# Attention followed by a gated convolution FFN on one core: a fixed order of the lead-in on three engines, weight casts in pieces, and the shifted V by DMA

## The chip, the core and the metric

The kernel runs on one core of a Trainium2 chip. The core has five engines that run side by side: TensorE (PE, matmuls; its weight loads are listed as PEld), VectorE (DVE), ScalarE (ACT), GpSimd (POOL) and SyncE (SP, which here only issues DMAs). The metric is the device time of one execution in microseconds, lower is better; a comparison takes the median of several runs.

## The reference

Eight batches of attention over a sliding window of 32 positions to each side, followed by a feed-forward layer with a convolution of width 3 along the sequence:

```python
# B, H, S, D = 8, 8, 576, 64;  d_model = 512, d_ff = 1024
scores = q @ k.T / sqrt(D)                    # per batch and head
scores = where(abs(i - j) <= 32, scores, -1e9)
attn   = softmax(scores)
x      = (attn @ v)  as [B, S, H * D]
h      = maximum(x @ w_in, 0)                 # [B, S, 1024]
conv   = sum_k conv_w[k] * h shifted by k - 1 # along S
gate   = 1 / (1 + exp(-conv))
out    = (h * gate) @ w_out                   # float32 [8, 576, 512]
```

## The kernel before

The kernel is written as a list of jobs, each with a planned time and the jobs it must follow. `give_out` takes them in the order of the planned times and emits their instructions; a scheduler may then move instructions of an engine past each other, unless they are wrapped in `fixed`, which keeps the program's order. The planned times are thus an order, not a clock.

A batch has four pair groups of heads (`g`). For each two groups `job_tr` transposes q and k on TensorE (the two engines ACT and DVE copy the halves out of PSUM), `job_sc` makes the scores of one group in a score buffer of which there is one, ACT takes the exponential, and DVE multiplies with the band mask. `job_av` multiplies with V. Half of the key tiles of V start 64 rows further down, so there are two copies of V in SBUF: `ve`, cast from the load, and `vo`, the same rows shifted by 64 partitions. `job_xt` transposes the result to the FFN's input, `job_ph` is the projection with `w_in`, `job_pc` the convolution (three matmuls with diagonal matrices `diag_w`) and the gate, and `job_py` the output projection.

```python
fixed = tc.keep_in_program_order

class InOrder:
    on = False
    def __getattr__(self, name):
        def give(*args, **kwargs):
            ins = getattr(nc.vector, name)(*args, **kwargs)
            return fixed(ins) if self.on else ins
        return give

vector = InOrder()                      # DVE alone; on for planned times under T0 + 14

def cast(out_, in_):                    # all casts of inputs and weights: POOL, in order
    fixed(nc.gpsimd.tensor_scalar(
        out=out_, in0=in_, scalar1=1.0, scalar2=0.0, op0=ALU.mult, op1=ALU.add))

def cast_v(c):                          # in load_stream(b)
    cast(ve[:, c, :, 0:64], vst[:, c, :, :])
    if b == 0 and c > 0:                # batch 0: shifted on DVE, block by block
        vector.tensor_copy(vo[0:64, c - 1, :, :], ve[64:128, c - 1, :, :])
        vector.tensor_copy(vo[64:128, c - 1, :, :], ve[0:64, c, :, :])

def shift_v(b):                         # the other batches: after the last cast of V
    ve, vo = ve_pp[b % NLD], vo_pp[b % NLD]
    for p0, src in ((0, ve[64:128, 0:NBLK - 1]), (64, ve[0:64, 1:NBLK])):
        if b == 1:
            vector.tensor_copy(out=vo[p0:p0 + 64], in_=src)
        else:
            fixed(nc.scalar.dma_start(vo[p0:p0 + 64], src))

def load_weight(src, dst, rows, cast_):
    n = src.shape[1] // 2
    for x in (0, n):                    # two halves: a load of 1 MB, and one cast
        ...
        yield load, lambda x=x, st=st: cast_(dst[:, :, x:x + n], st[0])

def make_diag(m):                       # three 128x128 matrices of one block m of 128 channels
    for kk in range(3):
        vector.tensor_scalar(out=diag_w[:, kk, m, :], in0=ident,
                             scalar1=conv_w_sb[:, kk, m:m + 1], scalar2=None, op0=ALU.mult)

def job_sc(g):
    ...
    ps, last = slot_a(), slot_f()       # slot_a: the one score buffer (three PSUM banks)
    ...                                 # 18 matmuls
    nc.scalar.activation(attn[:, 0:x], ps[:, 0:x], AF.Exp, bias=0.0, scale=scale)
    nc.scalar.activation(attn[:, x:], last[:, 0:64], AF.Exp, bias=0.0, scale=scale)
    vector.tensor_tensor(out=attn, in0=attn, in1=mask, op=ALU.mult)
```

The parts of the plan that belong to the lead-in (`b` is the batch, `g` the pair group, `c` a block of 128 rows, `m` a block of 128 channels):

```python
T0, T1 = 22.0, 42.5
hidden(0, T0, 1.6, None)                # chunk 0: job_ph at T0 + 1.6 m, job_pc at T0 + 1.6 (m + 1.4)
...
at(("diag", m), T0 + 1.6 * m - 1.0, ...)
# batch 0: transposes of q, of k; scores; attention times V
t0, t1, t2, t3 = 5.8 + 1.35 * (g // 2) * 2, 7.2 + 1.35 * (g // 2) * 2, 8.4 + 2.0 * g, 16.2 + g
at(("xt", b, c), ... if b else 20.3 + 0.4 * c, ...)
at(("vo", b), x + y + 1.5, lambda b=b: shift_v(b), ("cast", b, NV - 1))
at(("w_in", i), 16.5 + 2.0 * i, cs, ...)
at(("w_out", i), 34.0 + i, cs, ...)
```

Of the kernel before, what the change touches and what calls it, by code (L numbers as in the profile page):

```python
# [17 lines left out]
def kernel(  # L18
# [58 lines left out]
    class InOrder:  # L77


        on = False  # L80

        def __getattr__(self, name):
            def give(*args, **kwargs):
                ins = getattr(nc.vector, name)(*args, **kwargs)  # L84
                return fixed(ins) if self.on else ins

            return give

    vector = InOrder()

# [41 lines left out]
    def shift_v(b):  # L132

        ve, vo = ve_pp[b % NLD], vo_pp[b % NLD]
        for p0, src in ((0, ve[64:128, 0:NBLK - 1]), (64, ve[0:64, 1:NBLK])):
            if b == 1:
                vector.tensor_copy(out=vo[p0:p0 + 64], in_=src)
            else:
                fixed(nc.scalar.dma_start(vo[p0:p0 + 64], src))

# [42 lines left out]
    def load_weight(src, dst, rows, cast_):  # L183

        n = src.shape[1] // 2
        for x in (0, n):
            st = {}

            def load(x=x, st=st):
                t_ = fpool.tile([128, rows * n], FP32, name="wst", tag="wst")  # L190
                st[0] = t_.rearrange("p (c f) -> p c f", c=rows)
                fixed(nc.sync.dma_start(
                    st[0], src.rearrange("(c p) f -> p c f", p=128)[:, :, x:x + n]
                ))

            yield load, lambda x=x, st=st: cast_(dst[:, :, x:x + n], st[0])

# [10 lines left out]
    def job_tr(g2, y):  # L208

        b, i = g2 // NPH, g2 % NPH  # L210
        nat = qkb_pp[b % NLD][y][i]
        to = []
        for g in (2 * g2, 2 * g2 + 1):
            if y == 0:
                t_ = apool.tile([128, S], BF16, name="qT", tag="qT", bufs=4)
                to.append(t_)
            else:
                t_ = kT_pp[g % NKT]
                to.append(t_[:, PAD:PAD + S])
            state["qk"[y], g] = t_  # L220

        small = b == 0
        for js in ((range(0, 4), range(4, 8), range(8, RP)) if small else (range(RP),)):
            j0, n = js[0], len(js)
            ps = slot_f() if small else slot_a()
            for j in js:
                nc.tensor.matmul(  # L227
                    ps[:, 128 * (j - j0):128 * (j - j0) + 128],
                    nat[:, j, :, :].rearrange("p e d -> p (e d)"),
                    ident, start=True, stop=True,  # L230
                )
            rows = ps[:, 0:128 * n].rearrange("p (j y x) -> p y x j", j=n, y=2)
            for x, copy in enumerate((nc.scalar.copy, vector.tensor_copy)):
                copy(
                    out=to[x].rearrange("p (x j) -> p x j", j=RP)[:, :, j0:j0 + n], in_=rows[:, x]
                )

    def job_conv_w():
        ps = slot_f()
        nc.tensor.matmul(ps[:, 0:3 * MB], conv_w24, ident24, start=True, stop=True)  # L240
        vector.tensor_copy(out=conv_w_sb.rearrange("p k m -> p (k m)"), in_=ps[:, 0:3 * MB])
# [8 lines left out]
    def job_sc(g):  # L250
        qT, kT = state.pop(("q", g)), state.pop(("k", g))
        ps, last = slot_a(), slot_f()
        for i in range(NT):
            for e, t in ((0, (i + NT - 1) % NT), (1, i)):
                nc.tensor.matmul(  # L255
                    last[:, 0:64] if e * t == NT - 1 else ps[:, col(e, t):col(e, t) + 64],
                    kT[64 * e:64 * e + 64, 64 * t:64 * t + 128],
                    qT[64 * e:64 * e + 64, 64 * t:64 * t + 64],
                    start=True, stop=True,
                )  # L260
        attn = apool.tile([128, 2 * S], BF16, name="attn", tag="attn", bufs=4)
        state["a", g] = attn
        x = 2 * S - 64
        nc.scalar.activation(attn[:, 0:x], ps[:, 0:x], AF.Exp, bias=0.0, scale=scale)  # L264
        nc.scalar.activation(attn[:, x:], last[:, 0:64], AF.Exp, bias=0.0, scale=scale)  # L265
        vector.tensor_tensor(out=attn, in0=attn, in1=mask, op=ALU.mult)

    def job_av(g):
# [7 lines left out]
        for e in range(2):  # L276
            for c in range(NBLK):
                for j in range(2):
                    t = min(2 * c + j, NT - 1)
                    nc.tensor.matmul(  # L280
                        pss[e][64 * j:64 * j + 64, 65 * c:65 * c + 65],
                        attn[:, col(e, t):col(e, t) + 64],
                        (ve if t % 2 == 0 else vo)[:, t // 2, head(pr, e), :],
                        start=True, stop=True,
                    )
# [6 lines left out]
        for e, (po, rec, to) in enumerate(outs):  # L292
            if b == 0 and e == 1 and pr < 3:
                for c in range(NBLK):
                    nc.scalar.activation(
                        to[:, c, :], po[:, c, 0:64], AF.Copy, bias=0.0, scale=rec[:, c:c + 1]
                    )
# [6 lines left out]
    def job_xt(b, c):  # L304
# [5 lines left out]
        for kc in range(KC):  # L310
            nc.tensor.matmul(  # L311
                ps[:, kc, 0:cols],
                xn[b][:, c, 2 * kc:2 * kc + 2, :].rearrange("p h d -> p (h d)"),
                ident[:, 0:cols], start=True, stop=True,
            )
        (vector.tensor_copy if b > 1 or c % 2 else nc.scalar.copy)(
            out=xT[b // 2][:, :, b % 2, 128 * c:128 * c + cols], in_=ps[:, :, 0:cols]
# [13 lines left out]
    def job_ph(c, m, halves=(0, 1)):  # L331
# [8 lines left out]
        for kc in range(KC):  # L340
            nc.tensor.matmul(  # L341
                ps[:, 0:n], w_in_sb[:, kc, m * 128:(m + 1) * 128], x_[:, kc, x0:x1],
                start=(kc == 0), stop=(kc == KC - 1),
            )
        if kind == 1:
            out_ = hT[:, m, :].rearrange("p (i x) -> p i x", i=2)
            for i in halves:
                o_ = out_[:, i, i:i + HW + 1]
                i_ = ps[:, (HW + 1) * (i - halves[0]):(HW + 1) * (i - halves[0]) + HW + 1]
                if halves == (0, 1):  # L350
                    continue
                nc.scalar.activation(o_, i_, AF.Relu, bias=0.0, scale=0.5)
            if halves == (0, 1):
                base = hT[:, m, 0:HW + 1]
                both = bass.AP(base.tensor, base.offset, [list(base.ap[0]), [HW + 3, 2], [1, HW + 1]])
                nc.scalar.activation(
                    both, ps[:, 0:n].rearrange("p (i x) -> p i x", i=2), AF.Relu, bias=0.0, scale=0.5
                )
        else:
            o0 = 1 if kind == 0 else 0  # L360
            nc.scalar.activation(hT[:, m, o0:o0 + n], ps[:, 0:n], AF.Relu, bias=0.0, scale=0.5)  # L361

    def job_pc(c, m, halves=(0, 1)):
# [14 lines left out]
        for kk in range(3):  # L378
            nc.tensor.matmul(  # L379
                ps[:, 0:n], diag_w[:, kk, m, :], taps(kk), start=(kk == 0), stop=(kk == 2)  # L380
            )
        tn = spool.tile([128, CH], FP32, name="tn", tag="tn")
        nc.scalar.activation(tn[:, 0:n], ps[:, 0:n], AF.Tanh, bias=0.0, scale=1.0)  # L383
        vector.scalar_tensor_tensor(
# [8 lines left out]
    def job_py(c, i):  # L393

        ps = slot_f()
        for m in range(MB):
            nc.tensor.matmul(  # L397
                ps, gT[c][:, m, 128 * i:128 * i + 128], w_out_sb[:, m, :],
                start=(m == 0), stop=(m == MB - 1),
            )  # L400
        y_sb = spool.tile([128, d_model], FP32, name="y_sb", tag="y_sb", bufs=4)
        nc.scalar.copy(out=y_sb, in_=ps)  # L402
        r0 = c * CH + 128 * i
# [16 lines left out]
    def give_out():  # L420
# [9 lines left out]
        while ready:  # L430
            _, _, key = heapq.heappop(ready)
            vector.on = plan[key][0] < T0 + 14.0
            plan[key][1]()
# [7 lines left out]

    T0, T1 = 22.0, 42.5
    start = {0: T0, 1: T1}
# [21 lines left out]
    for m in range(MB):  # L465
        at(("diag", m), T0 + 1.6 * m - 1.0, lambda m=m: make_diag(m), ("conv_w",))
    at(("conv_w",), 7.0, job_conv_w)
# [26 lines left out]
    for g in range(NG):  # L494
# [4 lines left out]
        if b == 0:  # L499
            t0, t1, t2, t3 = 5.8 + 1.35 * (g // 2) * 2, 7.2 + 1.35 * (g // 2) * 2, 8.4 + 2.0 * g, 16.2 + g  # L500
        else:
# [9 lines left out]
    for b in range(B):  # L511
        t, d = pair[b * NP + NP - 1]
        for c in range(NBLK):
            at(("xt", b, c), t + (2.0 + 0.06 * c) * d if b else 20.3 + 0.4 * c, lambda b=b, c=c: job_xt(b, c),
               *[("av", b * NP + i) for i in range(NP)],
               *[("ph", (b // 2 - 2) * 3 + 2, m, None) for m in range(MB)])
        t0 = pair[b * NP][0]
        for i, (ld, cs) in enumerate(load_stream(b)):
            if b == 0:
                x, y = -20.0, 20 + (4.3 + 1.35 * i if i < NP else 9.8 + 1.1 * (i - NP))  # L520
            elif b == 1:
# [3 lines left out]
            else:  # L525
                x, y = t0 - P - 3.0 + i * P / NV, 4.5
            at(("load", b, i), x, ld if b else lambda: None, ("load", b, i - 1),
               *[("cast", b - 1, j) for j in range(NV)],
# [8 lines left out]
    for i, (ld, cs) in enumerate(load_weight(moe_w_in, w_in_sb, KC, cast)):  # L537
        at(("w_in load", i), -1.0, ld, *[("load", 0, j) for j in range(NV)])
        at(("w_in", i), 16.5 + 2.0 * i, cs, ("w_in load", i))
    for i, (ld, cs) in enumerate(load_weight(moe_w_out, w_out_sb, MB, cast)):  # L540
# [33 lines left out]
```

The softmax here doesn't subtract the row's maximum and nothing guards it: scores larger than these inputs give would overflow.

## Time and profile before

| | |
|---|---|
| median of 3 runs | 286.14 us (284.77 to 286.53) |
| span of the profiled execution | 282.2 us |
| PE busy | 246.8 us, 87% |
| DVE busy | 181.5 us, 64% |
| ACT busy | 175.9 us, 62% |
| POOL busy | 77.1 us, 27% |
| shift copies of V on DVE (`vo<-ve`) | 10, 290 to 2282 ns |
| shift DMAs of V on ACT's queue | 12, median 5.3 us from issue to landing |

How to read the profile: it is one execution, taken by the hardware profiler, and its times are microseconds from the start of the span. A group of instructions is written as line, engine, operation, output<-input, shape of each (partitions x elements) and count. In a timeline the first two numbers are the start and the length, and a bracket holds the idle time of the engine ahead of the group and what ended it. A table by stage has for each engine its busy time and, in brackets, its count of instructions; after the engines come TensorE's granted clock (1.00 is full speed), the share of the DMA engines and the rate in GB/s. L84 is the helper through which all DVE work of the jobs goes, so DVE's operations are told apart by their tiles; L109 is the cast on POOL. A matmul's end is modelled, so a busy PE is not PE at its peak.

### The profile page before, as it was taken

The page shows a single profiled execution, that of the slowest core. Times are in us where ns is not written, and L with a number is a line of the kernel's source. Part 1 is how long each engine was busy: PE and PEld are TensorE (multiplying, and loading weights), DVE is VectorE, ACT ScalarE, POOL GpSimd, SP SyncE. Part 2 cuts the span into 40 slices and gives each one's busy share as a digit, 9 for nine tenths or more (in the row PEclk, how much of TensorE's full clock was granted, in tenths as well). Part 3 has the DMA queues.
Part 4 walks back from the last instruction along what each step waited for, and adds up shares of the span by engine and source line. Part 5 has one row for each costly group of instructions (what it writes and reads, how often), then busy time and mean ns, then how long its engine had stood idle before and what let it go on. Part 6 is the DMA issues. An engine that isn't in the chain of part 4 may idle for free.

```text
span 282.2 us, 6681 instructions
## 1 busy us (share of the span) xinstructions
PE 246.8 (87%) x2652; PEld 152.2 (54%) x2682; DVE 181.5 (64%) x394; ACT 175.9 (62%) x370; POOL 77.1 (27%) x84
## 2 busy tenths in 40 slices
PE   1756767877999898999989999999989999999994
PEld 1535433656665554666555555565555655555551
DVE  5687989795465888486556767596656555733330
ACT  2755672565676666677765577766755677557652
POOL 5657738661026221043113412332200000000000
PEclk9999995797999999999999999999999999999999
DMA  6999999781687742784649564954240102011022
GB/s 231 253 329 360 210 365 256 193 280 32 171 207 239 199 114 66 231 272 118 148 95 310 156 161 131 306 165 114 65 115 37 39 37 78 37 39 74 37 78 112
DMA packets 55555, 45.58 MB, mean 162 GB/s; under 512 B 38860, under 2 KB 40932, under 8 KB 55524
## 3 DMA queue, kind: packets, MB, share of 16 engines
q1 hardware_dynamic: 54528, 41.95, 50.7%
q10 hardware_dynamic: 996, 3.21, 4.9%
q8 instruction: 21, 0.34, 0.6%
q14 instruction: 10, 0.08, 0.1%
HBM read 32.52 MB, written 9.44 MB: 149 GB/s over the span
## 4 chain that ended last, share of the span: by engine, by line
PE 70%; DVE 19%; ACT 5%; DMA 3%; issue 2%; SPq 1%; POOL 0%; DVEq 0%; ACTq 0%
PE pf L397 21%; PE pf L341 20%; PE pf L379 14%; PE pa L227 5%; PE pf L280 4%; DVE attn L84 3%; DVE xT L84 3%; DVE gT L84 3%; DMA kst<-in_k_dram 3%; DVE vo L84 3%; PE pa L255 3%; DVE diag_w L84 2%; ACT attn L264 2%; PE pf L311 2%; DVE xn L84 2%
## 5 line engine op out<-in xcount | busy, mean ns | idle before, releaser
L84 DVE SCALAR_TENSOR_TENSOR gT<-tn,hT 128x384 bf16<-128x384 f32 (+1 forms) x104 | 60.2, 587 | 43.2 <-ACT tn L383 42.9
L341 PE MATMUL pf<-xT,w_in_sb 128*128 128x385 bf16 (+2 forms) x416 | 81.3, 322 | 3.7 <-DVE xT L84 2.2
L379 PE MATMUL pf<-hT,diag_w 128*128 128x384 bf16 (+1 forms) x312 | 66.0, 320 | 2.6 <-DVE rec L84 1.5
L397 PE MATMUL pf<-w_out_sb,gT 128*128 128x512 bf16 x258 | 66.4, 380 | 1.6 <-issue 0.2
L383 ACT ACTIVATE tn<-pf 128x384 f32<-128x384 f32 (+1 forms) x104 | 49.0, 472 | 12.4 <-PE pf L379 11.8
L341 PEld LDWEIGHTS <-w_in_sb 128*128 128x128 bf16 x416 | 38.8, 100 | 27.1 <-DVE xT L84 2.0
L109 POOL TENSOR_SCALAR ve<-vst 128x512 bf16<-128x512 f32 x40 | 28.6, 719 | 60.8 <-DMA vst<-in_v_dram 37.7
L402 ACT COPY y_sb<-pf 128x512 f32<-128x512 f32 x36 | 21.1, 586 | 38.2 <-PE pf L397 35.8
L397 PEld LDWEIGHTS <-gT 128*128 128x128 bf16 x288 | 27.7, 98 | 29.3 <-issue 0.3
L361 ACT ACTIVATE hT<-pf 128x385 bf16<-128x385 f32 x64 | 31.8, 497 | 14.0 <-PE pf L341 13.4
L379 PEld LDWEIGHTS <-diag_w 128*128 128x128 bf16 x312 | 28.2, 99 | 20.9 <-issue 1.8
L264 ACT ACTIVATE attn<-pa 128x1088 bf16<-128x1088 f32 x32 | 34.5, 1079 | 7.2 <-PE pf L255 3.8
L84 DVE TENSOR_TENSOR attn<-attn,mask 128x1152 bf16<-128x1152 bf16 x32 | 27.1, 846 | 7.8 <-ACT attn L265 5.8
L109 POOL TENSOR_SCALAR qb<-qst 128x1152 bf16<-128x1152 f32 x16 | 19.3, 1204 | 35.6 <-DMA qst<-in_q_dram 32.5
L84 DVE TENSOR_TENSOR xn<-pf,rec 128x320 bf16<-128x320 f32 x61 | 27.8, 482 | 0.8 <-DVE rec L84 0.2
L84 DVE CAST xT<-pf 128x512 bf16<-128x512 f32 (+1 forms) x34 | 20.4, 634 | 9.6 <-PE pf L311 9.6
L109 POOL TENSOR_SCALAR kb<-kst 128x1152 bf16<-128x1152 f32 x16 | 19.1, 1194 | 19.1 <-DMA kst<-in_k_dram 12.2
L280 PEld LDWEIGHTS <-attn 128*64 128x64 bf16 x640 | 14.7, 119 | 16.5 <-issue 8.8
L280 PE MATMUL pf<-ve,attn 128*64 128x65 bf16 x384 | 19.2, 207 | 5.0 <-DVE attn L84 3.6
L255 PEld LDWEIGHTS <-kT 64*128 64x128 bf16 x576 | 12.7, 98 | 13.5 <-issue 6.7
L280 PE MATMUL pf<-vo,attn 128*64 128x65 bf16 x256 | 17.2, 207 | 3.0 <-DVE vo L84 3.0
L84 DVE RECIPROCAL rec<-pf 128x5 f32<-128x5 f32 x64 | 10.4, 181 | 14.1 <-PE pf L280 13.6
(54 smaller groups left out, 206.4 us busy)
## 6 DMA issues: line engine op xcount, KB each, us to landing
qst<-in_q_dram SPq DMA_DIRECT2D x16, 576.0 KB, 6.4
kst<-in_k_dram SPq DMA_DIRECT2D x16, 576.0 KB, 7.6
out_dram<-y_sb SPq DMA_DIRECT2D x36, 256.0 KB, 2.2
vst<-in_v_dram SPq DMA_DIRECT2D x24, 256.0 KB, 4.6
vo<-ve ACTq DMA_DIRECT2D x12, 260.0 KB, 5.3
vst<-in_v_dram SPq DMA_DIRECT2D x16, 192.0 KB, 4.6
wst<-in_moe_w_in_dram SPq DMA_DIRECT2D x2, 1024.0 KB, 8.3
wst<-in_moe_w_out_dram SPq DMA_DIRECT2D x2, 1024.0 KB, 9.5
```

Source lines behind the costliest of these rows:

```text
L84: ins = getattr(nc.vector, name)(*args, **kwargs)
L109: fixed(nc.gpsimd.tensor_scalar(out=out_, in0=in_, scalar1=1.0, scalar2=0.0, op0=ALU.mult, op1=ALU.add))
L227: nc.tensor.matmul(ps[:, 128 * (j - j0):128 * (j - j0) + 128], nat[:, j, :, :].rearrange("p e d -> p (e d)"), ident, start=True, stop=True,)
L255: nc.tensor.matmul(last[:, 0:64] if e * t == NT - 1 else ps[:, col(e, t):col(e, t) + 64], kT[64 * e:64 * e + 64, 64 * t:64 * t + 128], qT[ ...
L264: nc.scalar.activation(attn[:, 0:x], ps[:, 0:x], AF.Exp, bias=0.0, scale=scale)
L280: nc.tensor.matmul(pss[e][64 * j:64 * j + 64, 65 * c:65 * c + 65], attn[:, col(e, t):col(e, t) + 64], (ve if t % 2 == 0 else vo)[:, t // 2 ...
L341: nc.tensor.matmul(ps[:, 0:n], w_in_sb[:, kc, m * 128:(m + 1) * 128], x_[:, kc, x0:x1], start=(kc == 0), stop=(kc == KC - 1),)
L361: nc.scalar.activation(hT[:, m, o0:o0 + n], ps[:, 0:n], AF.Relu, bias=0.0, scale=0.5)
L379: nc.tensor.matmul(ps[:, 0:n], diag_w[:, kk, m, :], taps(kk), start=(kk == 0), stop=(kk == 2))
L383: nc.scalar.activation(tn[:, 0:n], ps[:, 0:n], AF.Tanh, bias=0.0, scale=1.0)
L397: nc.tensor.matmul(ps, gT[c][:, m, 128 * i:128 * i + 128], w_out_sb[:, m, :], start=(m == 0), stop=(m == MB - 1),)
L402: nc.scalar.copy(out=y_sb, in_=ps)
```

## The change

It has three parts. The helper that keeps the program's order is now used for TensorE, ACT and DVE alike, for all jobs with a planned time under T0 + 14, and the plan of the lead-in is written anew: the scores of batch 0's first two groups stand ahead of the transposes of the second two, three of the diagonal matrices are made early, the others later. The cast of each half of a weight is cut into four pieces of 128x512 elements. And the shifted V of all batches but the first comes by DMA on SP's queue, where batch 1 had it from DVE and the others from ACT's queue. The aim of the first part is a lead-in whose order is chosen and not left to the scheduler; of the second, that a weight's cast does not occupy POOL in one long operation; of the third, that neither DVE nor ACT's queue carries the shift.

```diff
+        def __init__(self, engine):
+            self.engine = engine
+
         def __getattr__(self, name):
-            ...
+            do = getattr(self.engine, name)
+            return (lambda *args, **kwargs: fixed(do(*args, **kwargs))) if InOrder.on else do
-    vector = InOrder()
+    vector, scalar, tensor = InOrder(nc.vector), InOrder(nc.scalar), InOrder(nc.tensor)
 ...  (in the jobs nc.tensor becomes tensor, and nc.scalar scalar)
         for p0, src in ((0, ve[64:128, 0:NBLK - 1]), (64, ve[0:64, 1:NBLK])):
-            if b == 1:
-                vector.tensor_copy(out=vo[p0:p0 + 64], in_=src)
-            else:
-                fixed(nc.scalar.dma_start(vo[p0:p0 + 64], src))
+            fixed(nc.sync.dma_start(vo[p0:p0 + 64], src))
 ...  (load_weight)
-            yield load, lambda x=x, st=st: cast_(dst[:, :, x:x + n], st[0])
+            def casts(x=x, st=st):
+                step = 512 // n
+                for c in range(0, rows, step):
+                    cast_(dst[:, c:c + step, x:x + n], st[0][:, c:c + step])
+
+            yield load, casts
 ...  (the plan)
-    T0, T1 = 22.0, 42.5
+    T0, T1 = 23.0, 43.0
-        at(("diag", m), T0 + 1.6 * m - 1.0, lambda m=m: make_diag(m), ("conv_w",))
+        at(("diag", m), (8.8, 9.0, 11.7)[m] if m < 3 else T0 + 1.6 * m - 1.5, lambda m=m: make_diag(m), ("conv_w",))
-            t0, t1, t2, t3 = 5.8 + 1.35 * (g // 2) * 2, 7.2 + 1.35 * (g // 2) * 2, 8.4 + 2.0 * g, 16.2 + g
+            t0, t1 = ((6.0, 7.5), (10.5, 12.2))[g // 2]
+            t2, t3 = (9.4, 10.4, 14.7, 16.2)[g], 18.0 + 0.8 * g
-  ("xt", b, c): 20.3 + 0.4 * c   for batch 0
+  ("xt", b, c): 21.5 + 0.3 * c
-                x, y = -20.0, 20 + (4.3 + 1.35 * i if i < NP else 9.8 + 1.1 * (i - NP))
+                x, y = -20.0, 20 + ((4.9, 6.4, 8.8, 10.9)[i] if i < NP else 12.1 + 1.25 * (i - NP))
-            at(("load", b, i), x, ld if b else lambda: None, ("load", b, i - 1),
+            at(("load", b, i), x, ld if b else lambda: None, ("load", b, i - 1), *[("vo", 1)][:b - 1],
-        at(("w_in", i), 16.5 + 2.0 * i, cs, ("w_in load", i))
+        at(("w_in", i), 17.2 + 1.0 * i, cs, ("w_in load", i))
```

The term added to `("load", b, i)` keeps the loads of batches 2 and later behind batch 1's shift on the queue.

## The prediction

> **What bounds the kernel now.** I first read the page's slices, to see where TensorE isn't full, and then the busy times by stage.
>
> ```profile
> PE   1756767877999898999989999999989999999994
> PEclk9999995797999999999999999999999999999999
> ...
> 30.00:40.00 10.00, 9.04 (x87) 5.22 (x88) 8.33 (x22) 7.45 (x16) 4.79 (x7) 1.00 1.03 287
> 40.00:52.00 12.00, 8.41 (x74) 4.82 (x74) 11.48 (x18) 3.99 (x8) 8.38 (x6) 0.60 0.88 250
> 52.00:70.00 18.00, 13.33 (x201) 11.13 (x201) 13.16 (x28) 12.07 (x29) 8.89 (x11) 0.89 0.58 177
> 70.00:283.00 213.00, 200.52 (x2075) 119.01 (x2102) 126.54 (x260) 136.72 (x279) 36.49 (x40) 1.00 0.46 131
> ```
>
> A slice is 7 us. From the fourteenth slice (92 us) on TensorE is at eight or nine tenths, and in the stage from 70 us it is busy for 200.5 of 213 us at full clock. What follows 70 us is TensorE's own work, and nothing in the change makes that smaller. So the change can win only before 70 us: each microsecond by which TensorE gets its full stream earlier is a microsecond off the end. The columns after the stage's length are PE, PE's weight loads, DVE, ACT, POOL, then the clock and the DMA share. The stage 40 to 52 stands out: DVE 11.48 of 12 us, ACT nearly idle, the clock at 0.60.
>
> Next the timeline of DVE and of POOL in that stage:
>
> ```profile
> 39.31 3.01 DVE L84 COPY vo<-ve 64x2080 bf16<-64x2080 bf16 x2
> 42.35 0.76 DVE L84 TENSOR_TENSOR attn<-attn,mask 128x1152 bf16<-128x1152 bf16 x1
> 43.02 4.12 DVE L84 TENSOR_SCALAR diag_w<-ident,conv_w_sb 128x128 bf16<-128x128 bf16 x3
> 47.06 0.55 DVE L84 SCALAR_TENSOR_TENSOR gT<-tn,hT 128x384 bf16<-128x384 f32 x1
> ```
> ```profile
> 39.62 2.15 POOL L109 TENSOR_SCALAR w_out_sb<-wst 128x2048 bf16<-128x2048 f32 x1 [3.94 <-DMA wst<-in_moe_w_out_dram]
> 42.60 2.27 POOL L109 TENSOR_SCALAR w_out_sb<-wst 128x2048 bf16<-128x2048 f32 x1 [0.83 <-DMA wst<-in_moe_w_out_dram]
> 44.84 1.15 POOL L109 TENSOR_SCALAR qb<-qst 128x1152 bf16<-128x1152 f32 x1
> 45.95 1.15 POOL L109 TENSOR_SCALAR kb<-kst 128x1152 bf16<-128x1152 f32 x1
> ```
>
> Three diag_w operations take 0.57 us elsewhere (at 37.29) and 4.12 us here; each waits out one POOL cast. The second shift copy takes 2.28 us for the same reason (its median over all shapes is 0.44). TensorE's attention-times-V for batch 1 can start only at 43.16, after the shift copies and the mask product.
>
> Last, the timeline of DVE before the first projection matmul (at 29.96 us):
>
> ```profile
> 19.20 2.86 DVE L84 COPY vo<-ve 64x520 bf16<-64x520 bf16 x4
> ...
> 27.41 0.69 DVE L84 CAST xT<-pf 128x512 bf16<-128x512 f32 x1 [0.94 <-PE pf L311]
> 28.02 1.29 DVE L84 TENSOR_SCALAR diag_w<-ident,conv_w_sb 128x128 bf16<-128x128 bf16 x3
> 29.23 0.68 DVE L84 CAST xT<-pf 128x512 bf16<-128x512 f32 x1
> ```
>
> Three diag_w operations stand between two xT copies that TensorE waits for. One of the four shift copies took 1.89 us (chain of work, at 19.85) beside the w_in cast of 19.70 to 21.60.
>
> **What the Trainium skill says.** "SBUF — State Buffer", section "Who interferes with whom": VectorE and GpSimd share one pair of SBUF ports, and a copy or tensor-scalar in a two-port mode and a GpSimd operation exclude each other for a whole instruction. The trace agrees: 1.89 us for a diag_w operation whose median is 0.246, beside casts of 2.27 us. It follows that a cast in four pieces makes VectorE wait for a piece, not for the whole. "TensorE: Matmul & The Clock Gate", "What's actually happening": after some 3.4 us of idling the array's clock is halved until it has been busy as long. The trace has it: TensorE is all but idle from 39.57 to 43.16 and the clock is 0.50 in 44 to 52. "DMA: Bandwidth & Descriptors", "Queues, rings and completion order": in a queue each DMA engine takes its work in ring order, and changes between queues by packets. So a shift issued on SP stands behind the loads issued before it, where one on ACT's queue would take turns with them. The trace of before can't show this for the shift, since batch 1 used DVE; the ACT-queue shifts landed in 3.1 to 7.2 us, median 5.3.
>
> **The change, part by part.**
>
> *Lead-in order.* Now the first score group's exponential runs 10.36 to 11.55, and the second's starts only at 14.03, since the next pair group's transposes and copies come between. Put first, the second group's 17 matmuls (0.66) start when the score buffer is free at 11.44, and its exponential at about 12.2, ending 13.5. Then six ACT copies of some 0.36 (2.2) give 15.7, scores and exponential of the third group 2.0 give 17.7, the fourth 1.7: 19.4, against 20.1 now. That is 0.7 on ACT. DVE has less to win. From 13.5 it must still do a mask product (0.76), six copies (2.2), three diag_w (0.57), eight shift copies (eight times 0.46, 3.7) and two more products (1.5): 8.7, so 22.2, plus something for contention, against 22.85 now. All of attention-times-V needs the last shift, so this brings 0 to 0.6. The three diag_w groups moved into DVE's early idle time leave the xT copies alone: the second xT copy moves from 29.23 to about 28.1, 1.1 earlier. First projection matmul: 29.96 less 1.2, about 28.8.
>
> *Weight casts in pieces.* A w_in half now takes 1.90. A 128x512 cast takes 0.62 (V's at 35.05), so four take 2.5: POOL loses 0.6 per half, 1.2 for w_in, and the casts of batch 1 move about 0.6 later, less what DVE no longer takes from them. For w_out nothing waits at once. On DVE the worst wait for one operation falls from some 2 us to 0.6: the diag_w group of 4.12 falls to at most 3 x (0.25 + 0.62) = 2.6, and it stands earlier, ahead of the w_out casts, so that I expect 0.6 to 1.0.
>
> *Shifted V by SP.* Takes 3.01 from DVE at 39.31. The last V cast of batch 1 ends at 33.81 + 1.87 = 35.68, about 36.2 with the slower POOL. Two issues (0.54 each by the ACT-queue rows) and 5.3 to landing would give 42.0 or so; behind the w_out loads, whose second half now lands at 42.6, it may be 43. I take 42.3, against 43.16 for attention-times-V now: 0.9 earlier. TensorE will stand before it, done with its earlier work by about 38 instead of 39.5, so the 1.2 of the lead-in is not added: the gate eats it.
>
> *After the gate.* In 40 to 52 us TensorE does, at full clock, 9 transposes (0.66), two attention-times-V groups (1.2), three conv groups (1.5), one full projection (0.66) and two half ones (0.7), some transposes (0.3): 5.0 us of work in 12. Of the 7 lost, some 2.5 lie before 43.16 and 4.5 after. Those 4.5 are diag_w waits and the halved clock. The diag_w waits go; the clock stays halved for a while, since the wait ahead of the gate is over 3.4 us again. I give back 2.6 of the 4.5. In 52 to 70 batch 1's scores, now late from the same DVE queue (its xT copies end at 69), come earlier, so that TensorE has fewer holes: 18 us hold 13.3 busy, of which I give back 1.2.
>
> *Later batches.* Twelve issues leave ACT's queue (12 x 0.54 = 6.5 us), but ACT is 62% busy and seldom ends a wait: 0.3.
>
> Sum: 0.9 + 2.6 + 1.2 + 0.3 = 5.0. Predicted: 286.14 - 5.0 = 281.1 us.
>
> **The rivals.**
>
> *The transfer takes the copy's place as the wait.* The shift waits on SP for the last V cast, and in its rings for 2 MB of w_out; and with TensorE's order fixed, attention-times-V can't be overtaken by the scores and transposes now run at 39.1 to 41.5. For it: the DMA share is 1.0 there, and w_out lands at 42.6. Then TensorE idles from 38 to 44 or 45, the clock stays halved, and the gain of the gate turns to a loss of 1 to 2; about 284 to 287. Against it: DVE isn't held any more, so what follows runs faster.
>
> *TensorE fills earlier than I think.* If the shift lands by 40, the wait falls below the clock's window and most of the 7 us come back, with 2 to 3 more in 52 to 70: 276 to 278.
>
> *The SP queue as a new block.* Output stores and loads stand behind a shift that waits for a cast. For it: the queue keeps the program's order. Against it: y_sb has four buffers and outputs come some 6 us apart, and the shift stands after its casts by the plan. At worst 1 to 2 us per batch for six batches: 290. Unlikely.
>
> **Range and chances.** The central sum has two soft terms, the gate (from -2 to +3) and what follows it (1 to 5). Together, with 1 us of scatter between runs, I take 276.8 to 285.8. The 2% line is 280.4, just under my value: 0.43 faster, 0.53 within 2%, 0.04 slower.
>
> **What would show it.** Right: the first projection matmul at 28 to 29.3; the second exponential at about 12.2; no diag_w group over 2.6 us; DVE under 9 of 12 us in 40 to 52; batch 1's first attention-times-V at 41 to 43, with vo's landing as its releaser; a stage after 70 us that is as dense as now. Wrong: that matmul group after 44 us, waiting for the DMA of vo, or a clock of 0.5 for more than 8 us (first rival); new waits of TensorE or of ACT's y_sb copies after 80 us (third); a first projection after 29.5 (DVE bounds the lead-in).

## The result and the profile after

The changed kernel takes 279.14 us in the median (four runs, 276.6 to 281.7), the kernel before 285.45 us beside it; the ratio is 0.9702 with a 95% interval of 0.963 to 0.9773. (The comparison leaves disturbed runs out, so a ratio here isn't always the quotient of two medians.) Six more runs, taken with the last experiments, have a median of 277.35 us and a ratio of 0.9717 (0.9677 to 0.9757).

The page's slices and the table by stage of the changed kernel, to be laid beside those of before:

```profile
PE   0746975886999999999999999999999999999994
PEclk9999996899999999999999999999999999999999
...
40.00:52.00 12.00, 6.76 (x70) 4.44 (x70) 8.76 (x16) 3.93 (x9) 8.91 (x11) 0.72 1.12 303
52.00:70.00 18.00, 14.32 (x237) 11.19 (x237) 14.31 (x30) 12.37 (x32) 8.78 (x10) 1.00 0.79 206
70.00:283.00 213.00, 197.85 (x2064) 117.33 (x2088) 128.37 (x260) 135.81 (x278) 38.01 (x40) 1.00 0.46 129
```

In 40 to 52 us DVE has gone from 11.48 to 8.76 busy and the clock from 0.60 to 0.72, and yet TensorE does less there than before, 6.76 instead of 8.41. What the 12 us hold now is one wait. TensorE's timeline in the changed kernel, its rows with a wait (L87 is the helper that keeps the order; it now carries the lines of three engines):

```profile
28.28 2.73 PE L87 MATMUL pf<-xT,w_in_sb 128*128 128x385 bf16 x8 [0.66 <-DVE xT L87]
...
41.10 0.22 PE L87 MATMUL pf<-ve,attn 128*64 128x65 bf16 x1 [0.94 <-DVE attn L87]
44.19 0.22 PE L87 MATMUL pf<-vo,attn 128*64 128x65 bf16 x1 [2.88 <-DMA vo<-ve]
51.25 0.66 PE L87 MATMUL pa<-ident,kb 128*128 128x128 bf16 x9 [1.33 <-DVE qT L87]
```

The first row is the start of the projections, 29.96 before. The row at 44.19 is the one that I call the gate: batch 1's attention times V, 43.16 before, now stands still for the DMA of `vo` and starts a microsecond later. SP's queue of the changed kernel shows what is ahead of that DMA:

```profile
31.36 2.00 SPq L189 DMA_DIRECT2D wst<-in_moe_w_out_dram  x2
35.12 1.53 SPq L136 DMA_DIRECT2D vo<-ve  x2
36.71 0.58 SPq L103 DMA_DIRECT2D qst<-in_q_dram  x1
```

And DVE's diagonal matrices, none of which takes 4.12 for three any more:

```profile
38.14 1.36 DVE L87 TENSOR_SCALAR diag_w<-ident,conv_w_sb 128x128 bf16<-128x128 bf16 x3
...
40.97 0.92 DVE L87 TENSOR_SCALAR diag_w<-ident,conv_w_sb 128x128 bf16<-128x128 bf16 x3
...
47.66 1.45 DVE L87 TENSOR_SCALAR diag_w<-ident,conv_w_sb 128x128 bf16<-128x128 bf16 x3
```

Where did the gain arise? The 36 output copies on ACT (`y_sb`, one per 128 rows of the result) are a clock of the kernel's progress. The table has the starting times of the first and the last from the timelines of the profiled runs, and how long some stretches between two copies take (those of the experiments below are already included):

```
output copy                       1st    36th   1st-36th | 4th-8th  12th-13th  13th-21st  21st-22nd
before                          71.34  278.52   207.19   |  30.20     8.22       52.54      8.22
changed                         69.38  271.15   201.77   |  28.33     7.76       50.74      7.76
changed, second trace (e12)     73.72  277.23   203.51   |  28.80     7.76       52.00      7.76
e1: before, later on SP         71.02  274.35   203.33   |  29.31     6.75       52.13      6.75
e3: changed, later on ACT       71.54  275.97   204.44   |  28.59     9.21       50.27      9.20
e10: changed, spare on ACT      68.56  273.54   204.98   |  28.59     9.20       50.81      9.20
e11: order alone                70.80  275.94   205.14   |  28.59     9.20       50.91      9.21
e2: all but the third part      70.20  275.72   205.52   |  28.59     9.21       51.28      9.20
e9: changed, b1 on DVE          70.83  273.20   202.36   |  28.84     7.76       50.53      7.76
e8: w_out behind shift          65.26  268.57   203.32   |  28.85     7.76       51.47      7.76
```

In its first trace the changed kernel is 2.0 us ahead at the first output and 7.4 at the last: more than two thirds of its lead comes after the first output, where I had expected almost nothing. Its second trace, a run of 282.69 us, is 2.4 behind at the first output and 1.3 ahead at the last. So the way to the first output differs by over 4 us between two runs of the same kernel (in the second the gate is at 46.0 and the clock 0.90 in 52 to 70 us, where it is 1.00 in the first), and what follows it is 5.4 us shorter than before in the one and 3.7 in the other. That later gain, and the gate, are what the experiments are about. The theory I went in with after reading both traces: the later gain comes from ACT, which no longer issues DMAs. The rivals: it is carried over from the new lead-in, or it is whatever the scheduler makes of the jobs that aren't pinned.

### The profile page after: what moved, and what is told of

Read it like the earlier page. It is cut to its first block, busy times and chain, and to the rows that moved or that the text cites. A ratio compares the mean times of both kernels' runs of the same rounds, so it can differ in the third digit from the quotient of the medians.

```text
span 274.9 us, 6658 instructions
## 1 busy us (share of the span) xinstructions
PE 243.0 (88%) x2654; PEld 149.9 (55%) x2682; DVE 179.0 (65%) x392; ACT 174.4 (63%) x370; POOL 81.2 (30%) x96
## 4 chain that ended last, share of the span: by engine, by line
PE 69%; DMA 11%; DVE 8%; SPq 4%; ACT 3%; issue 3%; POOL 1%
PE pf L399 22%; PE pf L343 19%; PE pf L381 14%; DMA kst<-in_k_dram 5%; PE pa L229 4%; PE pf L282 4%; DMA vst<-in_v_dram 4%; SPq L95 3%; DMA vo<-ve 3%; PE pa L257 3%; PE pf L313 2%; DVE xT L318 2%; DVE attn L268 2%; DVE gT L386 1%; DVE gT L87 1%
## 5 line engine op out<-in xcount | busy, mean ns | idle before, releaser
L343 PE MATMUL pf<-xT,w_in_sb 128*128 128x385 bf16 (+2 forms) x380 | 73.4, 315 | 2.3 <-DVE xn L301 1.4
L381 PE MATMUL pf<-hT,diag_w 128*128 128x384 bf16 (+1 forms) x288 | 58.7, 313 | 0.7 <-ACT hT L354 0.6
L404 ACT COPY y_sb<-pf 128x512 f32<-128x512 f32 x36 | 21.1, 586 | 42.5 <-PE pf L399 40.2
L343 PEld LDWEIGHTS <-w_in_sb 128*128 128x128 bf16 x380 | 33.9, 98 | 21.9 <-DVE xn L301 2.0
L266 ACT ACTIVATE attn<-pa 128x1088 bf16<-128x1088 f32 x26 | 28.0, 1076 | 5.6 <-PE pf L257 4.8
L268 DVE TENSOR_TENSOR attn<-attn,mask 128x1152 bf16<-128x1152 bf16 x26 | 22.3, 857 | 7.2 <-ACT attn L267 6.6
L301 DVE TENSOR_TENSOR xn<-pf,rec 128x320 bf16<-128x320 f32 x52 | 23.4, 480 | 0.4
L358 ACT ACTIVATE hT<-pf 128x386 bf16<-128x386 f32 x24 | 11.8, 499 | 5.4 <-PE pf L343 5.2
L282 PEld LDWEIGHTS <-attn 128*64 128x64 bf16 x520 | 10.6, 111 | 8.3 <-issue 6.0
L282 PE MATMUL pf<-ve,attn 128*64 128x65 bf16 x312 | 13.8, 197 | 0.5 <-DVE attn L268 0.3
L257 PE MATMUL pa<-qT,kT 64*128 64x64 bf16 x442 | 12.5, 191 | 0.9 <-DVE kT L236 0.9
```

The lines of the kernel that those rows point to most:

```text
L282: tensor.matmul(pss[e][64 * j:64 * j + 64, 65 * c:65 * c + 65], attn[:, col(e, t):col(e, t) + 64], (ve if t % 2 == 0 else vo)[:, t // 2, h ...
L301: vector.tensor_tensor(out=to, in0=po[:, :, 0:64], in1=rec[:, :, None].broadcast_to([128, NBLK, 64]), op=ALU.mult,)
L343: tensor.matmul(ps[:, 0:n], w_in_sb[:, kc, m * 128:(m + 1) * 128], x_[:, kc, x0:x1], start=(kc == 0), stop=(kc == KC - 1),)
L381: tensor.matmul(ps[:, 0:n], diag_w[:, kk, m, :], taps(kk), start=(kk == 0), stop=(kk == 2))
```

## The experiments

A run's time varies more than most of these parts are worth, so I read the medians together with the profile of the stage concerned. In the table "before" is the kernel before, measured beside it.

| kernel | median us | range us | before us | ratio (95%) |
|---|---|---|---|---|
| e11 order alone | 281.06 | 278.69 to 283.17 | 284.49 | 0.9842 (0.9797 to 0.9886) |
| e7 pieces alone | 283.89 | 280.32 to 286.39 | 284.49 | 0.9876 (0.9828 to 0.9923) |
| e5 third part alone | 280.37 | 278.99 to 284.20 | 284.49 | 0.9841 (0.9807 to 0.9876) |
| e1 third part, later batches alone | 281.07 | 277.28 to 284.02 | 284.38 | 0.9842 (0.98 to 0.9884) |
| e2 all but the third part | 279.11 | 275.54 to 281.21 | 284.38 | 0.9739 (0.9688 to 0.9791) |
| e4 all but the pieces | 279.02 | 276.73 to 280.14 | 284.38 | 0.9817 (0.9774 to 0.9861) |
| e3 all, later batches on ACT | 280.64 | 277.91 to 281.58 | 284.38 | 0.9869 (0.982 to 0.9917) |
| e10 all, spare shift on ACT | 281.53 | 279.00 to 283.19 | 284.34 | 0.9889 (0.9835 to 0.9942) |
| e6 all, batch 1 on ACT | 278.95 | 276.51 to 280.63 | 284.34 | 0.9802 (0.9749 to 0.9855) |
| e9 all, batch 1 on DVE | 279.17 | 278.26 to 280.97 | 284.34 | 0.981 (0.9763 to 0.9857) |
| e12 all, once more | 277.35 | 275.08 to 283.06 | 284.49 | 0.9717 (0.9677 to 0.9757) |
| e8 all, w_out behind the shift | 273.60 | 271.91 to 275.28 | 284.34 | 0.9611 (0.9563 to 0.9658) |

### The later gain: e1, e3, e10

e1 is the kernel before with one word changed:

```diff
-                fixed(nc.scalar.dma_start(vo[p0:p0 + 64], src))
+                fixed(nc.sync.dma_start(vo[p0:p0 + 64], src))
```

> The kernel before, with the shift of batches 2 to 7 on SP's queue; batch 1 keeps DVE, nothing else is changed. Theory ACT queue (the 5.4 us that the changed kernel gains after 70 us come from ACT no longer issuing twelve DMAs ahead of its copies): the first output copy stays at 71.3, the lead grows to 4.5 to 5.5 us by 220 us; time 280 to 281.5. Rival carried lead (the rewritten lead-in puts the later attention jobs ahead of the projections and so takes out the later holes): within 1 us of before. Rival order (the scheduler arranges the jobs after the lead-in anew whenever anything is altered, and the gain is that arrangement's): anything from -4 to +4, with the order of the jobs on TensorE differing.

Measured: 281.07, and the lead over before grows from 0.3 at the first output to 4.2 at the last, a little under the theory's 4.5 to 5.5. The table of output copies shows two single steps, at the 13th and the 22nd, of 1.47 us each, in a kernel that has nothing of the new lead-in. So a carried lead isn't needed for these.

e3 goes the other way, the changed kernel with batches 2 to 7 back on ACT's queue:

```diff
-            fixed(nc.sync.dma_start(vo[p0:p0 + 64], src))
+            fixed((nc.sync if b == 1 else nc.scalar).dma_start(vo[p0:p0 + 64], src))
```

> The changed kernel, with the shift of batches 2 to 7 back on ACT's queue; batch 1 stays on SP. Theory ACT queue: the lead-in as in the changed kernel (first output copy 69.4), but the lead of 2.0 stops growing: 281.5 to 283. Rivals carried lead: 276.5 to 278, no difference. Rival order: a difference of either sign, with the jobs' order on TensorE differing after 60 us.

Measured: 280.64, a little under the theory's range, and the lead over before doesn't stop growing: what follows the first output is still 2.8 us shorter than before. So ACT's issues are at most a part of the later gain. The stretches from 12th to 13th and from 21st to 22nd output take 9.2 instead of 7.8. What happens in the first of them is seen in ACT's timeline of e3 (ACTq is ACT's queue of DMA issues):

```profile
143.93 0.47 ACTq L136 DMA_DIRECT2D vo<-ve  x1
144.04 0.52 ACT L363 ACTIVATE hT<-pf 128x385 bf16<-128x385 f32 x1
144.50 0.66 ACTq L136 DMA_DIRECT2D vo<-ve  x1
145.19 0.64 ACT L236 CAST qT<-pa 128x576 bf16<-128x576 f32 x1 [0.63 <-PE pf L343]
```

and in TensorE's, also of e3:

```profile
147.38 0.65 PE L381 MATMUL pf<-hT,diag_w 128*128 128x384 bf16 x3 [0.75 <-DVE rec L292]
148.57 0.66 PE L229 MATMUL pa<-ident,kb 128*128 128x128 bf16 x9 [0.55 <-DVE qT L236]
```

The q copy stands behind two issues. It starts 3.4 us after the output copy of 141.79; in the changed kernel, at the same place, it comes 2.6 us after that of 139.40:

```profile
142.03 0.66 ACT L236 CAST qT<-pa 128x576 bf16<-128x576 f32 x1
```

DVE's half of the copy comes later still. First DVE in e3, then at the same place in the changed kernel:

```profile
144.50 0.55 DVE L386 SCALAR_TENSOR_TENSOR gT<-tn,hT 128x384 bf16<-128x384 f32 x1
146.51 0.20 DVE L292 RECIPROCAL rec<-pf 128x5 f32<-128x5 f32 x1 [1.46 <-PE pf L282]
147.78 0.75 DVE L236 CAST qT<-pa 128x576 bf16<-128x576 f32 x1
```
```profile
142.10 0.55 DVE L386 SCALAR_TENSOR_TENSOR gT<-tn,hT 128x384 bf16<-128x384 f32 x1
142.72 0.76 DVE L236 CAST qT<-pa 128x576 bf16<-128x576 f32 x1
```

TensorE, which needs the one score buffer free for k's transposes, stands still twice, 1.3 us together. The profile puts the wait down to DVE ("DVE rec", "DVE qT"), which was also so in the kernel before. ACT's mean load told nothing of it.

The scheduler has a hand in this. In the changed kernel DVE takes its half of the copy right after the gate product; in e3 it stands still for 1.46 us for attention times V and takes the copy only after that group's results, though ACT's half is done at 145.83. DVE's order differs at the same two places, and at some others, between the kernel before and e1 and between e10 and the changed kernel; it is one and the same in both traces of the changed kernel. The issues themselves hold ACT's copy up by 0.63 us. How much of the 1.45 is that delay, and how much the order that the scheduler makes of it, is not shown, since no run holds the order and moves the issues alone.

e10 asks whether it is the issue on ACT or the arrival of the data that counts: everything as in the changed kernel, and each later shift issued once more by ACT, into a tile that nothing reads.

```diff
             fixed(nc.sync.dma_start(vo[p0:p0 + 64], src))
+            if b > 1:
+                fixed(nc.scalar.dma_start(spare[p0:p0 + 64], src))
```

> The changed kernel; each shift of batches 2 to 7 is issued a second time, on ACT's queue, into a spare tile that nothing reads. Theory ACT queue (the issue on ACT itself is the cost): the lead over before stops growing in 140 to 220 us, TensorE busy for 75.5 to 77.5 of the 80 us there as with the shift on ACT's queue, instead of 78.8; time 1.5 to 3 us over the changed kernel. Rival landing (the shift's arrival is what differs between the queues): no difference from the changed kernel in 140 to 220, where PE stays at 78.5 to 79.2.

Measured: 281.53, and again 9.2 and 9.2. TensorE's stage from 140 to 220 us, first of the changed kernel, then of e10:

```profile
140.00:220.00 80.00, 78.79 (x897) 47.70 (x901) 57.20 (x114) 55.96 (x112) 17.65 (x18) 1.00 0.56 153
```
```profile
140.00:220.00 80.00, 76.54 (x858) 45.83 (x856) 56.75 (x110) 53.44 (x108) 18.25 (x18) 1.00 0.62 169
```

The data that are used come by SP in both. So the stretches take 9.2 wherever ACT issues, whatever the issue moves, and the rival of the arrival falls; the scheduler's order stays in, as said. Of the six pairs of issues two cost time, 1.45 us each, 2.9 together. That isn't 2.9 of the gain over before: the new order alone makes each of the two stretches a microsecond longer (9.2 in e11 for 8.2), so between the two kernels they give 0.5 each.

### The gate: e6, e8, e9

e8 moves the loads of `w_out` behind batch 1's shift on SP:

```diff
-        at(("w_out load", i), 0.0, ld, *[("load", 1, j) for j in range(NV)], ("w_in", i))
+        at(("w_out load", i), 0.0, ld, *[("load", 1, j) for j in range(NV)], ("w_in", i), ("vo", 1))
```

> The changed kernel, with the two loads of w_out (2 MB) issued on SP behind batch 1's shift instead of ahead of it. Theory ring order (the shift waits in the queue for the 2 MB ahead of it): batch 1's shift lands 2 to 5 us after its issue at 35 to 36.5, so its attention times V starts at 39.5 to 41 instead of 44.2, the clock stays at 1.0 or drops for under 5 us, and the first output copy comes 2 to 4 us earlier unless w_out, now later by 1 to 2 us, isn't cast by then; time 1 to 4 us under the changed kernel: 274 to 278 against a median of 279. Rival V cast (the shift waits for the last cast of V, not for the ring): attention times V moves by less than 1 us, time unchanged.

Measured: 273.60, the fastest kernel of the study, with all six runs below the changed kernel's lower median of 277.35; the two were not measured side by side, but the intervals of their ratios to before (0.9563 to 0.9658, and 0.9677 to 0.9757) don't overlap. SP's queue and TensorE's gate in e8:

```profile
34.52 1.17 SPq L136 DMA_DIRECT2D vo<-ve  x2
35.74 2.04 SPq L189 DMA_DIRECT2D wst<-in_moe_w_out_dram  x2
```
```profile
39.60 0.22 PE L87 MATMUL pf<-ve,attn 128*64 128x65 bf16 x1 [0.17 <-DVE attn L87]
```

Attention times V starts at 39.60 and no longer waits for a DMA. The stage of 40 to 52 us in e8:

```profile
40.00:52.00 12.00, 9.38 (x169) 6.92 (x161) 10.84 (x28) 8.83 (x21) 7.34 (x10) 1.00 1.04 345
```

169 matmuls against 70, at full clock. The first output comes at 65.3, 4.1 earlier than in the changed kernel's first trace, although `w_out` is cast later now, from 43.9 to 50.8, in front of the next batch's casts, and the clock drops to 0.81 in 52 to 70 instead. At the last output 2.6 are left. Where the rest goes is not shown: the largest part is lost from the 13th to the 21st output, where e8 lies between the two traces of the changed kernel.

e6 puts batch 1's shift on ACT's queue, where nothing is ahead of it, though `w_out` was issued earlier on SP's:

```diff
-            fixed(nc.sync.dma_start(vo[p0:p0 + 64], src))
+            fixed((nc.scalar if b == 1 else nc.sync).dma_start(vo[p0:p0 + 64], src))
```

> The changed kernel, with batch 1's shift on ACT's queue and the later batches' on SP. Theory ring order: on a queue of its own the shift takes turns with w_out's packets and lands 3 to 7 us after its issue, at 39.5 to 42.5; attention times V 2 to 4 us earlier than 44.2. Against it works that ACT stands still at the issue until the last V cast (35.5 to 36.2), 1 to 3 us of projections' copies. Time 277 to 280. Rival V cast: attention times V as in the changed kernel, and time the same or 1 to 2 us over it.

Measured: 278.95, and the ring-order theory missed. In ACT's timeline of e6 the issues are at 36.38 and 37.01; in TensorE's:

```profile
45.48 0.26 PE L87 MATMUL pf<-vo,attn 128*64 128x65 bf16 x1 [4.39 <-DMA vo<-ve]
```

A queue of its own didn't help: with the shift on SP behind `w_out` and the new order, the gate is at 43.8 to 46.0 in five traces, and 45.48 lies within that. The packets in the traces show what is ahead of it (a shift packet is 4160 bytes, one of `w_out` 1024):

```
                       last w_out packet   shift issued     shift packets
changed, shift on SP         40.73         35.12, 36.20    39.93 to 42.94
e6, shift on ACT             40.32         36.38, 37.01    40.68 to 44.44
e8, shift ahead of w_out     46.64         34.52, 35.15    35.71 to 38.14
```

In e6 the first shift packet moves 4.3 us after its issue and 0.36 us after the last packet of `w_out`, on another queue. So the shift comes behind the 2 MB issued earlier, whichever queue it is on, and the rival of the V cast falls with e8. But `w_out` is not all that is ahead in e6. With the shift gone from SP's queue, batch 2's loads of q and k are issued from 32.49 on, and 246 of their packets (2304 bytes each) move before the shift's first one. From then on both queues move: from 40.68 to 44.44 it is 127 packets of the shift on ACT's queue and 232 of those loads on SP's. Why the shift didn't move beside `w_out` and did beside these loads is not shown.

e9 gives batch 1 back to DVE and leaves the rest of the change:

```diff
+            if b == 1:
+                vector.tensor_copy(out=vo[p0:p0 + 64], in_=src)
+            else:
                 fixed(nc.sync.dma_start(vo[p0:p0 + 64], src))
```

> The changed kernel, with batch 1's shift on DVE as before and the later batches' on SP. With whole casts gone, a DVE shift copy waits 0.6 us at most for POOL; attention times V starts at 42 to 43 (42.5 in the kernel without the third part). Theory ACT queue: this keeps the later gain, so 276.5 to 278.5, 0.5 to 2 us under the changed kernel. If DVE's time is what counts in 40 to 52 us, it is 1 to 3 us over it.

Measured: 279.17, over the expected 276.5 to 278.5. The gate is at 41.50, 2.7 earlier than by SP, and the two DVE copies take 1.42 together. But DVE then holds up what follows: three of the diagonal matrices take 2.84 beside the pieces of `w_out`, and k's transposes wait 2.95 for the q copy; the first output comes at 70.8, while in e6, with the gate 4 us later, it comes at 68.3. So an earlier gate alone doesn't bring an earlier first output. Between SP and DVE for batch 1 the times don't decide.

### The parts one by one: e11, e7, e5, e2, e4, e12

e11 is the new order alone (the changed kernel with the old `shift_v` and whole casts):

> The kernel before with the new lead-in order alone: casts whole, shifts as before. The kernel with order and pieces took 279.1, and undoing the pieces in the changed kernel moved its median by 0.1. If the pieces do nothing for the total: 279 to 281.5. If the pieces are what keeps DVE's shift of batch 1 and the diagonal matrices short, it is 282 to 284, with a DVE operation of over 1.8 us in 38 to 48 us.

Measured: 281.06, by its time as if the pieces did nothing. Its profile says otherwise: batch 1's gate is at 47.2, 4 us later than before, and the longest shift copy took 2281 ns. It wins elsewhere. After the first output it is 2.1 us shorter than before. The stretch from the fourth to the eighth output is 28.6 us in e11, 28.3 in the changed kernel and 30.2 before, where TensorE waits 1.7 us by name for DVE's mask products and results; with the old order (e7) it stays at 30.2. From the 13th to the 21st it wins 1.6 more and 0.5 after the 22nd, and it loses 2.0 in the two stretches that e1 shortens. So about 2 us of the later gain come with the new order; which job's place does it is not shown.

e7 is the pieces alone:

```diff
-            yield load, lambda x=x, st=st: cast_(dst[:, :, x:x + n], st[0])
+            def casts(x=x, st=st):
+                step = 512 // n
+                for c in range(0, rows, step):
+                    cast_(dst[:, c:c + step, x:x + n], st[0][:, c:c + step])
+
+            yield load, casts
```

> The kernel before with the casts in pieces alone. By the prediction's working: the diag_w groups' waits fall from 1.9 to 0.9 us each at most and the longest shift copy from 2.3 to about 1.2; attention times V of batch 1 at 42 instead of 43.2, 1 to 3 us off the time: 281.5 to 283.5. Rival (pieces do nothing for the total): 283.5 to 285.5.

Measured: 283.89, with a ratio of 0.9876; by the median this is the range of the rival, that the pieces do nothing. The shift copies and the gate (42.3) are as expected, the size in the whole is small. DVE's shift copies (minimum, median and longest, ns), from the view of the tile, first of e11, then of e7:

```profile
L87 DVE COPY vo<-ve x10: 289/291/2281, 16.7 to 39.5; 64x520 bf16<-64x520 bf16 x8, 64x2080 bf16<-64x2080 bf16 x2
```
```profile
L84 DVE COPY vo<-ve x10: 289/591/1002, 16.9 to 40.1; 64x520 bf16<-64x520 bf16 x8, 64x2080 bf16<-64x2080 bf16 x2
```

e5 is the third part alone, batch 1 included:

```diff
-            if b == 1:
-                vector.tensor_copy(out=vo[p0:p0 + 64], in_=src)
-            else:
-                fixed(nc.scalar.dma_start(vo[p0:p0 + 64], src))
+            fixed(nc.sync.dma_start(vo[p0:p0 + 64], src))
```

(and the shift ahead of batch 2's loads, as in the change)

> The kernel before with the third part alone, batch 1 included. Theory ring order and ACT queue together: batch 1's attention times V at 44 to 46, later than the 43.2 of before; 2.9 us won in two steps between 140 and 220 us by the free ACT queue; in all 281 to 284, no better than the 281.1 of the kernel with the later batches alone on SP. If batch 1's shift off DVE is a gain: 278 to 280.5.

Measured: 280.37, against 281.07 for e1, not measured side by side: batch 1's share can't be told from nothing. Its trace, of the longest of its runs (284.20), has the gate at 48.7, later than the 44 to 46 expected and the latest of all, and again the two stretches at 6.8.

e2 is the changed kernel without the third part, e4 the one without the pieces; their edits are those of e5 and e7 the other way.

> The changed kernel without its third part: batch 1 shifted by DVE, the others by ACT's queue; new lead-in order and casts in pieces stay. Theory ACT queue: first output copy near 69 to 70, no growth of the lead afterwards, 283 to 284 (1.5 to 2.5 under before). Rival carried lead: 277 to 279, as the whole change. If batch 1's shift on DVE is no loss once the casts are in pieces, its attention times V starts before 43, earlier than the 44.2 of the changed kernel.

Measured: 279.11, where the theory of ACT's queue had 283 to 284: a miss. Its trace has both stretches at 9.2, as the theory says, and yet three of its runs took 275.5 to 277.4, no more than the whole change (the other three 280.9 to 281.2), and its ratio of 0.9739 can't be told from the 0.9717 of e12. e9, which differs from e2 only in having the later shifts on SP and should be 2.9 faster, took 279.17. So the two stretches are shortened in every trace that takes the issues from ACT, but between these two kernels the times don't show it, and why is open. e2's gate, at 42.5, is 1.7 earlier than that of the changed kernel, as expected of DVE. Beside e11 (gate at 47.2, whole casts) it suggests what the pieces are good for: they matter as long as DVE makes the shift.

> The changed kernel with each weight half cast whole, its second part undone. By the prediction the pieces keep DVE's waits at 0.6 us in place of some 2: undone, the last shift copies of batch 0 end about 1 us later, the first projection comes at 28.8 to 29.3 instead of 28.3, and some diag_w groups take over 2 us; time 0.5 to 1.5 us over the changed kernel, 277.5 to 278.5. Rival: the pieces only cost POOL 0.6 us a half, and undone the time is 0 to 0.6 lower.

Measured: 279.02. The projections start at 29.2 instead of 28.3, as expected (29.2 in e11 too; 27.9 to 28.8 in the eight traces with the new order and pieces), but no diag_w operation took over 1.14 us and the time can't be told from the changed kernel's.

The changed kernel again, beside e11, e7 and e5:

> The changed kernel once more, beside the parts. Its runs so far spread from 276.6 to 281.7, with the batch 1 shift's landing and TensorE's clock in 40 to 70 us as what differs. Expected 279, from 276.5 to 282, ratio to before 0.975 to 0.985.

Measured: 277.35, from 275.08 to 283.06. No single part reaches its ratio of 0.972: alone they give 0.984, 0.988 and 0.984. The first two together do (e2).

## Why the prediction was right, and where it wasn't

The total was right: 281.1 predicted, 276.8 to 285.8 as the range, 279.14 measured. A gain of less than 2% was put as likelier (0.53) than the 3.0% that came (0.43). Step by step:

- **Lead-in order.** Right in mechanism, a little small. The second exponential was to start at about 12.2 and starts at 12.34. The projections were to start 1.2 earlier and start 1.7 earlier. DVE's last mask product and shift copies went faster than I allowed for, as did the two xT copies without the diagonal matrices between them.
- **Weight casts in pieces.** Right: groups of three diagonal matrices take at most 1.45 where I allowed 2.6, and DVE is busy for 8.76 of the 12 us, under the 9 that I named. In the time of the whole it is the smallest part when made alone.
- **Shifted V by SP.** The step that failed first. I put the gate at 42.3, 0.9 earlier; it is at 44.19, 1.0 later. The term mis-sized is the landing: I took 5.3 us from the ACT-queue shifts, and the second of these took about 8 (issued at 36.20, with the gate open at 44.19), because I gave the 2 MB of `w_out` 0.3 us (42.0 to 42.3) where they cost about 4: in e8, with them behind it, the second shift is issued at 35.15 and lands at 39.10. It is the first rival's mechanism, at the time that it named (44 to 45), but not with its sum.
- **After the gate.** 3.8 us were to come back by 70 us, with the gate 4.7. Measured at the first output: 2.0 in the first trace. With the gate 1.9 worse than assumed, this term is roughly 3.0 instead of 3.8 there; in the second trace, 2.4 behind at the first output, where the gate is at 46.0, it is about 0.5.
- **Later batches.** The step that failed most, and in the other direction: 0.3 predicted, 5.4 measured (3.7 in the second trace). "Nothing in the change makes that smaller" was wrong. I argued from ACT's mean load of 62%, though a queue's place in a chain was to be asked. In the traces of the parts what follows the first output is shorter than before by 3.9 with the later shifts on SP alone (e1), by 2.1 with the new order alone (e11) and by 0.4 with the pieces alone (e7). 2.9 of the 3.9 arise in two single places, where two issues stand ahead of the q copy. Whether the issues' own delay or the scheduler's order costs it, and which job's place in the new order wins the 2.1, stays open.
- **SP queue as a block.** It didn't come: nothing on TensorE waits for more than 0.5 us by name after 70 us.

So that the total fits is in part luck: 2.7 too much before 70 us and 5.1 too little after it make 2.4 in sum on the first pair of profiled runs.

## What to carry to other kernels

When a DMA is issued on an engine that also computes, look at what stands behind the issue in that engine's order, and at whether the other engines' orders change with it; with two issues of half a microsecond ahead of a PSUM copy a stretch took 1.45 us longer at two places, and the four other pairs cost 0.3 us together (e10). When a small transfer is on the path, ask what was issued ahead of it on any queue: moving 2 MB that nobody needed yet behind the half megabyte that TensorE waited for brought the ratio from 0.972 to 0.961. And read a gain at several points of the run, by an operation that repeats, and in more than one trace, before putting it down to the stage that was rewritten.

## What the runs showed of the hardware

Beside `w_out` the queues of SP and ACT did not take turns: in e6 a shift issued on ACT at 36.38 moved its first packet at 40.68, 0.36 us after the last of 2 MB that SP had issued from 30.44 to 32.40. Beside batch 2's loads both queues moved, 127 packets of the one and 232 of the other from 40.68 to 44.44. The first half differs from what the prediction took from the Trainium skill, "DMA: Bandwidth & Descriptors", section "Queues, rings and completion order", and the second agrees; which DMA engine moved a packet is not in the record, so the rule itself is neither shown nor refuted, and the measurement decides for this case.

The same kernel differs by several microseconds from run to run: the changed one from 275.08 to 283.06 in six runs, the one before from 282.41 to 288.73 in seventeen. Between the two traces of the changed kernel (69.4 and 73.7 at the first output) most of the difference lies before the first output.
